# A fused attention and expert kernel: five raw weight buffers, loads one block further ahead, and one more set of keys and values ahead of the weights

## The chip, the cores and the metric

The kernel runs on one core of a Trainium2 chip. The time is device microseconds of one execution; several executions are timed and their median is taken. A separate execution is recorded by the hardware profiler, and all rows below are from that one.

## The reference

Three layers follow each other, all in fp32. The first is an attention with 16 heads (2 batches of 8) of 512 local and 32 global positions; a local position sees the global ones and its neighbours within 32. The second is a dense layer with three weight matrices, of which the largest product counts, and an output matrix. The third sends each token to one of eight experts. Cut to what matters:

```
out_l = softmax(q_l @ [k_g, k_l].T / 8, |pos difference| <= 32) @ [v_g, v_l]
out_g = softmax(q_g @ [k_g, k_l].T / 8) @ [v_g, v_l]
x = rows(out_g, out_l)                          # 1088 x 512
h = maximum(maximum(x @ w1, x @ w2), x @ w3)    # 512 x 768 each, float64 in memory
x = h @ w_out
e = argmax(x @ w_gate); y = gate * (relu(x @ w1[e]) @ w2[e])
```

## The kernel before

Everything up to the dense layer runs in one loop that is written out by hand. The heads are worked on in 16 sets of two heads and half a sequence; each set has one tile of queries and keys (`qk`, from `dma_qk`) and one of values (`rawv`, from `dma_v`), each with five buffers. A set has two units of 128 queries, so there are 32 units. The loop runs over steps s from -2 on. A step does one part of several units: scores, maximum and exponentials of unit s+2, the transpose of unit s (`u_trans` on TensorE, and `u_thi`, its copy `ph` on ScalarE), the product with the values of unit s-1 (`u_pv`), and the transposed output of unit s-2 (`x_out`). Steps 1, 5, 9 and so on also do scores of global positions (`g_scores`). The scores have one buffer (`ps_s`), so those of the next unit wait for the maximum of the last. `SEQ` lists the order of these parts in a step; each engine takes its instructions in the order in which the loop writes them. `idles` gives the number of matmuls on zeros (`warm`) that a step adds for TensorE.

The dense layer's weights are float64 in memory and are read as raw blocks of 128 x 512 (`raww`, 18 of them, three for each slice f of 128 hidden columns; then 6 of `w_out`). `split64` turns a block into a high and a low fp32 part: L337 on ScalarE reads the block, then L339, L342 and L345 on VectorE, L349 on ScalarE writes the high part, L352 and L354 on VectorE (L354 is the last to read the block), then L355 and L356 on GpSimd. The generator `w_stream` loads and splits the blocks in order. It is moved on by `take`: each advance does one pass, seven advances make one block, and the table `w_steps` says how many advances a step makes, divided over the places w0, w1 and w2 of `SEQ`. From step 10 on the dense layer's first matmuls (`moe_first`, L454) are mixed in.

All transfers of this part are issued by SP, which takes them in the order of the program, and one whose buffer is not free yet holds up those behind it. Ahead of the loop go qk of sets 0 to 2 and v of sets 0 and 1. The loop issues qk and v of one more set in every even step.

Of the kernel before, what the change touches and what calls it, by code (L numbers as in the profile page):

```python
# [7 lines left out]
F32 = mybir.dt.float32  # L8
# [4 lines left out]
I32 = mybir.dt.int32  # L13
# [6 lines left out]
P = 128  # L20
# [30 lines left out]
def tile_block(ctx: ExitStack, tc: tile.TileContext, qk, qg, v, vo, vg, w123, w_out, w_gate, w1, w2, consts, out):  # L51
# [16 lines left out]
    wp = wps.enter_context(tc.tile_pool(name="wp", bufs=2, side="right"))  # L68
# [14 lines left out]
    def warm(n):  # L83

        if n:
            o = ps_mm.tile([P, 512], F32, tag="mm", name="warm")
        for _ in range(n):
            nc.tensor.matmul(o[0:32], lhsT=idle, rhs=idle.unsqueeze(1).to_broadcast([P, 16, 32]), start=True, stop=True)
# [6 lines left out]
    def dma_qk(m):  # L95
        K[m] = ap.tile([P, 256 + KU], F32, tag="qk", bufs=5, name=f"qk{m}")
        nc.sync.dma_start(K[m], qk[m])

    def dma_v(m):
        V[m] = ap.tile([P, 8, P], F32, tag="rawv", bufs=5, name=f"rawv{m}")  # L100
        nc.sync.dma_start(V[m].rearrange("p t c -> p (t c)"), v[m])
# [69 lines left out]
    def u_scores(n):  # L171
        m, u = divmod(n, 2)
        ps = ps_s.tile([P, 2, 512], F32, tag="s", name=f"s{n}")
        PS_[n] = ps
        for j in range(2):
            t = K[m][64 * j : 64 * j + 64]
            for g in range(4):
                a = 256 + 32 * (5 * u + g)
                nc.tensor.matmul(ps[32 * g : 32 * g + 32, j, 0:P], lhsT=t[:, u * P + 32 * g : u * P + 32 * g + 32], rhs=t[:, a : a + P], start=True, stop=True)  # L179

    def u_max(n):
        m, u = divmod(n, 2)
        half = SETS[m][1]
        mk = mask[:, 0 if half == 0 and u == 0 else (2 if half == 1 and u == 1 else 1), :]
        nm = ap.tile([P, 2], F32, tag="nm", bufs=4, name=f"nm{n}")
        if u == 0:
            SS[m] = ap.tile([P, 2, 4], F32, tag="ssum", bufs=3, name=f"ss{m}")
        ssum = SS[m][:, 0, 2 * u : 2 * u + 2]
        sm = sms[n % NSM]
        SM[n] = (sm, nm, ssum)  # L190
        ps = PS_[n]
        for j in range(2):
            nc.vector.tensor_tensor_reduce(sm[:, j], ps[:, j, 0:P], mk, scale=-0.125, scalar=3.0e38, op0=ALU.add, op1=ALU.min, accum_out=nm[:, j : j + 1])  # L193
# [9 lines left out]
    def u_recip(n):  # L203
        if n % 2:
            t = SS[n // 2]
            nc.vector.reciprocal(t[:, 0], t[:, 1])

    def u_trans(n):
        sm = SM[n][0]
        pt = ps_t.tile([P, 2, P], F32, tag="pt", name=f"pt{n}")  # L210
        for j in range(2):
            nc.tensor.transpose(pt[:, j], sm[:, j], ident)
        PT_[n] = [pt]

    def u_thi(n):
        ph = ap.tile([P, 2, P], F32, tag="ph", name=f"ph{n}")
        nc.scalar.copy(ph, PT_[n][0])
        PT_[n].append(ph)

    def u_pv(n):  # L220
        m, u = divmod(n, 2)
        po = ps_v.tile([P, 2, 64], F32, tag="pv", name=f"pv{n}")
        _, ph = PT_.pop(n)
        for j in range(2):
            for g in range(4):
                nc.tensor.matmul(po[32 * g : 32 * g + 32, j], lhsT=ph[:, j, 32 * g : 32 * g + 32], rhs=V[m][:, 4 * u + g, 64 * j : 64 * j + 64], start=True, stop=True)
        xq = ap.tile([P, 2, 64], F32, tag="xq", bufs=3, name=f"xq{n}")
        nc.vector.tensor_tensor(xq, po, SM.pop(n)[2].unsqueeze(2).to_broadcast([P, 2, 64]), op=ALU.mult)
        PV_[n] = xq
# [127 lines left out]

    def dma_w(src, name):
        if wide:
            raw = wp.tile([P, 512, 2], I32, tag="raww", bufs=3, name=name)  # L360
            nc.sync.dma_start(raw.rearrange("p n t -> p (n t)"), src.bitcast(I32))
        else:
            raw = wp.tile([P, 512], F32, tag="raww", bufs=3, name=name)
            nc.sync.dma_start(raw, src)
        return raw

# [10 lines left out]
    def w_stream():  # L377

        todo = [("w", f, i) for f in range(NF) for i in range(3)] + [("o", f, 0) for f in range(NF)]
        raw = {}  # L380

        def load(k):
            if k < len(todo):
                kind, f, i = todo[k]
                raw[k] = dma_w(w123[f, i] if kind == "w" else w_out[f * P : (f + 1) * P], f"raw{kind}{f}{i}")

        load(0)
        load(1)
        yield
        load(2)  # L390
        old = iter(())
        for k in range(len(todo) + 1):

            new = (split64 if wide else split32)(raw.pop(k), *todo[k]) if k < len(todo) else iter(())
            next(old, None)
            yield
            next(new, None)
            yield
            next(old, None)
            if k:  # L400
                load(k + 2)
            yield
            for _ in range(4):
                next(new, None)
                yield
            old = new
# [54 lines left out]
    def take(gen, n):  # L461
        for _ in range(n):
            if next(gen, StopIteration) is StopIteration:
                return False
        return True
# [110 lines left out]
    ws = w_stream()  # L576
    NSET = len(SETS)
# [6 lines left out]
    def moe_stream():  # L584
        for g, f, at in ORDER:
            for _ in moe_first(f, *(WIN1[g])):
                yield at if at < 99 else 99 + f / 10
# [14 lines left out]
    GDVE = 6  # L602
    MM = (7, 4, 2, 1)

    w_steps = {-2: 1, 1: 2, 2: 1, 3: 2, 4: 2, 5: 1, 6: 2, 7: 1, 8: 1, 9: 1, 10: 6, 11: 5, 12: 5, 13: 3, 14: 2, 15: 3, 16: 7, 17: 3, 18: 1, 19: 5, 20: 4, 21: 3, 22: 1, 24: 4, 26: 6, 27: 3, 28: 1, 29: 1, 30: 5, 31: 4, 32: 2, 33: 2}
    idles = {-2: 4, 0: 1, 4: 3, 6: 1, 9: 1, 10: 1, 11: 1}

    GQ = {17: (0, 0), 21: (0, 1), 28: (1, 0), 31: (1, 1)}
# [1 line left out]
    mstream = None  # L610
    dma_qk(2)
    dma_v(1)
    for s in range(-2, NU + 6):
        live, ahead = 0 <= s < NU, 0 <= s + 2 < NU
        if s == 10:
            mstream = Stream(moe_stream())
        pull = (lambda n: mstream.pull(n, s)) if mstream else (lambda n: None)
        nw = w_steps.get(s, 0)
        for c_ in SEQ[0 if s < 14 else 1].split():
            if c_ == "scores" and ahead:  # L620
                u_scores(s + 2)
            elif c_ == "trans" and live:
                u_trans(s)
                u_thi(s)
            elif c_ == "max" and ahead:
                u_max(s + 2)
            elif c_ == "recip" and 0 <= s + 1 < NU:
                u_recip(s + 1)
            elif c_ == "pv" and 0 <= s - 1 < NU:
                u_pv(s - 1)  # L630
            elif c_ == "out" and 0 <= s - 2 < NU:
                x_out(s - 2)
            elif c_ == "exp" and ahead:
                u_exp(s + 2)
            elif c_ == "idle":
                warm(idles.get(s, 0))
            elif c_ == "quad":
                if s in GQ:
                    globs.append(g_quad(*GQ[s]))
                globs = [g for g in globs if next(g, StopIteration) is not StopIteration]  # L640
            elif c_ == "glob" and ahead and s % 4 == 1:
                g_scores((s - 1) // 2)
            elif c_ == "gcopy" and ahead and s % 4 == 1:
                g_copies((s - 1) // 2)
            elif c_[0] == "w":
                take(ws, (nw + int(c_[1])) // 3)
            elif c_[0] == "m" and c_ != "max":
                pull(MM[int(c_[1])])

        if s % 2 == 0:  # L650
            m = (s + 6) // 2
            if 3 <= m < NSET:
                dma_qk(m)
            if 2 <= m - 1 < NSET:
                dma_v(m - 1)
        if s == 11:
            load_qg(1)
        if s + 1 in GQ:
            dma_vg(*GQ[s + 1])
        if s == 28:  # L660
            routing_start()
        if s == 30:
            nc.sync.dma_start(out.rearrange("(p i) (j c) -> p (i j) c", p=64, c=P), zero[0:64].unsqueeze(1).to_broadcast([64, NT * DM // 64 // P, P]))
    k = 0
# [20 lines left out]
    k = 0  # L685
# [161 lines left out]
    def load(j, k):  # L847

        if j < NJ:
            kw = {} if j < 2 else {"cond": nsp[j] > 0}  # L850
            if k < 4:
                nc.sync.dma_start(raw_of(j, k), w1v[bass.ds(ereg[j], 1), k].rearrange("a p f -> (a p) f"), **kw)
            else:
                nc.sync.dma_start(raw_of(j, k), w2v[bass.ds(ereg[j], 1), k - 4].rearrange("a p i f -> (a p) i f"), **kw)
# [485 lines left out]
```

## Time and profile before

| what | value |
|---|---|
| median of 3 runs | 327.69 us (327.64 to 328.4) |
| the profiled execution's own time | 329.9 us |
| its span, first to last instruction | 328.1 us |
| busy in the span: TensorE / VectorE / ScalarE / GpSimd | 309.8 / 235.7 / 181.3 / 148.6 us |
| mean granted TensorE clock | 0.974 of full |

The busy times are sums over stages with different limits. A TensorE row counts as busy for as long as its matmuls last, also where they last longer at a lower clock. The granted clock is given as a share of 2.4 GHz: 1.00 is that level and 0.50 is 1.2 GHz.

### The profile page before, as it was taken

The page shows a single profiled execution, that of the slowest core. Times are in us where ns is not written, and L with a number is a line of the kernel's source. Part 1 is how long each engine was busy: PE and PEld are TensorE (multiplying, and loading weights), DVE is VectorE, ACT ScalarE, POOL GpSimd, SP SyncE. Part 2 cuts the span into 40 slices and gives each one's busy share as a digit, 9 for nine tenths or more (in the row PEclk, how much of TensorE's full clock was granted, in tenths as well). Part 3 has the DMA queues.
Part 4 walks back from the last instruction along what each step waited for, and adds up shares of the span by engine and source line. Part 5 has one row for each costly group of instructions (what it writes and reads, how often), then busy time and mean ns, then how long its engine had stood idle before and what let it go on. Part 6 is the DMA issues. An engine that isn't in the chain of part 4 may idle for free. (4 is left out here: it accounts for less than half of the span.)

```text
span 328.1 us, 8717 instructions
## 1 busy us (share of the span) xinstructions
PE 309.8 (94%) x3280; PEld 264.3 (81%) x3280; DVE 235.7 (72%) x600; ACT 181.3 (55%) x457; POOL 148.6 (45%) x164
## 2 busy tenths in 40 slices
PE   7699868999999999999999999999899999999993
PEld 2355746778887899999999999999799777788762
DVE  2569988796688827998996001765879799999881
ACT  4668477768757522433443121346532689889860
POOL 1128958593674814676888000142000357831131
PEclk9869796999999999999999999999999999999999
DMA  7947777486253962243310011469756189999921
GB/s 243 413 162 274 262 262 249 160 303 212 80 193 125 193 155 66 66 130 128 130 64 3 0 65 64 146 237 346 231 170 256 53 312 399 395 405 399 390 81 32
DMA packets 27656, 64.43 MB, mean 196 GB/s; under 512 B 3018, under 2 KB 8140, under 8 KB 27600
## 3 DMA queue, kind: packets, MB, share of 16 engines
q1 hardware_dynamic: 26304, 59.91, 52.9%
q0 software_dynamic: 1296, 3.82, 3.1%
q8 instruction: 30, 0.49, 0.6%
q14 instruction: 26, 0.21, 0.2%
HBM read 60.95 MB, written 7.27 MB: 208 GB/s over the span
## 5 line engine op out<-in xcount | busy, mean ns | idle before, releaser
L454 PE MATMUL h<-xh,wh 128*128 128x256 f32 (+1 forms) x288 | 85.3, 296 | 0.5 <-DVE hA L441 0.5
L454 PE MATMUL h<-xl,wh 128*128 128x256 f32 (+1 forms) x288 | 85.5, 297 | 0.0
L454 PE MATMUL h<-xh,wl 128*128 128x256 f32 (+1 forms) x288 | 85.5, 297 | 0.0
L454 PEld LDWEIGHTS h<-xh,wh 128*128 128x128 f32 x288 | 55.6, 193 | 1.2 <-DVE hA L441 0.7
L454 PEld LDWEIGHTS h<-xh,wl 128*128 128x128 f32 x288 | 55.9, 194 | 0.8 <-issue 0.7
L454 PEld LDWEIGHTS h<-xl,wh 128*128 128x128 f32 x288 | 55.9, 194 | 0.4 <-issue 0.2
L444 POOL TENSOR_TENSOR hTl<-hA,hTh 128x256 fp32r<-128x256 f32 (+1 forms) x24 | 19.3, 806 | 55.8 <-ACT hTh L443 55.7
L239 POOL CAST xh<-xs 128x128 fp32r<-128x128 f32 x32 | 13.1, 408 | 37.0 <-ACT xs L237 37.0
L859 DVE TENSOR_TENSOR w2l<-rawb,w2h 128x1024 fp32r<-128x1024 f32 x23 | 27.3, 1214 | 2.0 <-ACT w2h L858 2.0
L443 ACT CAST hTh<-hA 128x256 fp32r<-128x256 f32 (+1 forms) x24 | 10.0, 416 | 33.6 <-DVE hA L441 33.5
L739 PE MATMUL x<-hTl,wo_h 128*128 128x256 f32 (+1 forms) x96 | 28.3, 294 | 0.0
L198 ACT ACTIVATE sm<-sm,nm 128x128 f32<-128x128 f32 x64 | 25.3, 399 | 5.3 <-DVE nm L193 5.2
L441 DVE TENSOR_TENSOR hA<-hA,h 128x256 f32<-128x256 f32 (+1 forms) x48 | 20.7, 432 | 10.3 <-PE h L454 8.5
L739 PE MATMUL x<-hTh,wo_l 128*128 128x256 f32 (+1 forms) x96 | 27.9, 291 | 0.0
L739 PE MATMUL x<-hTh,wo_h 128*128 128x256 f32 (+1 forms) x96 | 27.8, 289 | 0.0
L355 POOL TENSOR_TENSOR ct<-ct,wh 128x512 f32<-128x512 f32 x18 | 25.8, 1432 | 1.3 <-DVE ca L352 0.9
L193 DVE CUSTOM_DVE_ANT_0 sm<-s,mask 128x128 f32<-128x128 f32 x64 | 15.9, 285 | 13.8 <-PE s L179 9.2
L942 PE MATMUL py<-w2h,hhl 128*128 128x512 f32 x96 | 25.5, 395 | 0.2 <-DVE idsall L573 0.2
L356 POOL TENSOR_TENSOR wl<-ct,ca 128x512 fp32r<-128x512 f32 x18 | 24.3, 1352 | 2.0 <-DVE ca L354 0.7
L859 DVE TENSOR_TENSOR w1l<-rawb,w1h 128x1024 fp32r<-128x1024 f32 x20 | 23.7, 1216 | 1.7 <-ACT w1h L858 1.6
L858 ACT CAST w2h<-rawb 128x1024 fp32r<-128x1024 f32 x23 | 23.4, 1050 | 1.8 <-DMA rawb<-in_w_dram 1.8
L817 POOL DMA_INDIRECT xg<-x2d,idsall x7 | 14.8, 2120 | 16.0 <-PE xp L829 14.8
(232 smaller groups left out, 723.3 us busy)
## 6 DMA issues: line engine op xcount, KB each, us to landing
rawb<-in_w_dram SPq DMA_DIRECT2D x51, 512.0 KB
raww<-in_w_dram SPq DMA_DIRECT2D x18, 512.0 KB
rawv<-in_v_dram SPq DMA_DIRECT2D x16, 512.0 KB
qk<-in_qk_dram SPq DMA_DIRECT2D x16, 320.0 KB
rawo<-in_w_out_dram SPq DMA_DIRECT2D x6, 512.0 KB
rw<-in_w_dram SPq DMA_DIRECT2D x5, 512.0 KB
out_dram<-zero SPq DMA_DIRECT2D x1, 2176.0 KB
rawg<-in_vo_dram SPq DMA_DIRECT2D x4, 512.0 KB
```

What stands on the lines that cost most here:

```text
L193: nc.vector.tensor_tensor_reduce(sm[:, j], ps[:, j, 0:P], mk, scale=-0.125, scalar=3.0e38, op0=ALU.add, op1=ALU.min, accum_out=nm[:, j : j ...
L198: nc.scalar.activation(sm[:, j], sm[:, j], AF.Exp, bias=nm[:, j : j + 1], scale=-1.0, accum_out=ssum[:, j : j + 1])
L355: nc.gpsimd.tensor_tensor(tf, tf, hi.bitcast(F32), op=ALU.subtract)
L356: nc.gpsimd.tensor_tensor(lo, tf, b.bitcast(F32), op=ALU.add)
L441: nc.vector.tensor_tensor(hA[:, :T], hA[:, :T], ph[:, :T], op=ALU.max)
L444: nc.gpsimd.tensor_tensor(hl[:, f_, c0 : c0 + T], hA[:, :T], dst.bitcast(F32), op=ALU.subtract)
L454: nc.tensor.matmul(ph[:, :T], lhsT=w_[:, a], rhs=x_[:, c, c0 : c0 + T], start=n == 0, stop=n == 11)
L739: nc.tensor.matmul(po[:, :T], lhsT=w_[:, f, d * P : (d + 1) * P], rhs=h_[:, f_, c0 : c0 + T], start=k == 0, stop=k == 17)
L817: nc.gpsimd.indirect_dma_start(out=xg[t if j == 0 else j % 2], out_offset=None, in_=src, in_offset=bass.IndirectOffsetOnAxis(ap=IDS[j][0:n ...
L858: nc.scalar.copy(h_, raw_of(j, k))
L859: nc.vector.tensor_tensor(l_, raw_of(j, k), h_.bitcast(F32), op=ALU.subtract)
L942: nc.tensor.matmul(py[0:nt], lhsT=a[:, c, a0 : a0 + nt], rhs=w_[:, c], start=i == 0, stop=i == 23)
```

## The change

Raw weight blocks have five buffers where they had three. `w_stream` issues its first three loads in three advances, in place of two, and then loads block k+3 where it loaded k+2. The first two advances are made ahead of the loop: block 0 behind qk 2 and v 1, then qk 3 and v 2, then block 1. The loop issues qk and v of each later set one even step earlier. The first entries of `w_steps` are spread more evenly (2 advances in each of steps 2 to 9, 4 in 10 and 11); the first pass of block 0 comes with the fifth advance where it came with the third, and two advances are made ahead of the loop, so that by the end of step 11 both kernels have done the same passes, and each later step does what it did.

```diff
-            raw = wp.tile([P, 512, 2], I32, tag="raww", bufs=3, name=name)
+            raw = wp.tile([P, 512, 2], I32, tag="raww", bufs=5, name=name)
...
         load(0)
+        yield
         load(1)
         yield
         load(2)
+        yield
...
-            if k:
-                load(k + 2)
+            load(k + 3)
...
-    w_steps = {-2: 1, 1: 2, 2: 1, 3: 2, 4: 2, 5: 1, 6: 2, 7: 1, 8: 1, 9: 1, 10: 6, 11: 5, 12: 5, 13: 3, 14: 2, 15: 3, 16: 7, 17: 3, 18: 1, 19: 5, 20: 4, 21: 3, 22: 1, 24: 4, 26: 6, 27: 3, 28: 1, 29: 1, 30: 5, 31: 4, 32: 2, 33: 2}
+    w_steps = {1: 1, 2: 2, 3: 2, 4: 2, 5: 2, 6: 2, 7: 2, 8: 2, 9: 2, 10: 4, 11: 4, 12: 5, 13: 3, 14: 2, 15: 3, 16: 7, 17: 3, 18: 1, 19: 5, 20: 4, 21: 3, 22: 1, 24: 4, 26: 6, 27: 3, 28: 1, 29: 1, 30: 5, 31: 4, 32: 2, 33: 2}
...
     dma_qk(2)
     dma_v(1)
+    take(ws, 1)
+    dma_qk(3)
+    dma_v(2)
+    take(ws, 1)
...
-            m = (s + 6) // 2
-            if 3 <= m < NSET:
+            m = (s + 8) // 2
+            if 4 <= m < NSET:
                 dma_qk(m)
-            if 2 <= m - 1 < NSET:
+            if 3 <= m - 1 < NSET:
                 dma_v(m - 1)
```

SP's queue, from the last transfer but one that both kernels issue alike (`qk3` is the tile of set 3, `rawv2` that of set 2; `raww00` to `raww02` are raw blocks 0 to 2, `raww10` is block 3). Before:

```order
L101 DMA rawv1_147<-in_v_dram 128x1024
L361 DMA raww00_164<-in_w123_dram 128x1024
L361 DMA raww01_166<-in_w123_dram 128x1024
L97 DMA qk3_211<-in_qk_dram 128x640
L101 DMA rawv2_213<-in_v_dram 128x1024
L361 DMA raww02_254<-in_w123_dram 128x1024
L97 DMA qk4_299<-in_qk_dram 128x640
L101 DMA rawv3_301<-in_v_dram 128x1024
L97 DMA qk5_389<-in_qk_dram 128x640
L101 DMA rawv4_391<-in_v_dram 128x1024
L361 DMA raww10_485<-in_w123_dram 128x1024
L97 DMA qk6_489<-in_qk_dram 128x640
```

The same place of SP's queue with the change:

```order
L361 DMA raww00_149<-in_w123_dram 128x1024
L97 DMA qk3_151<-in_qk_dram 128x640
L101 DMA rawv2_153<-in_v_dram 128x1024
L361 DMA raww01_155<-in_w123_dram 128x1024
L97 DMA qk4_215<-in_qk_dram 128x640
L101 DMA rawv3_217<-in_v_dram 128x1024
L361 DMA raww02_261<-in_w123_dram 128x1024
L97 DMA qk5_303<-in_qk_dram 128x640
L101 DMA rawv4_305<-in_v_dram 128x1024
L361 DMA raww10_341<-in_w123_dram 128x1024
L97 DMA qk6_392<-in_qk_dram 128x640
```

qk 3 and v 2 have moved in front of block 1, and one pair of qk and v now stands between any two blocks.

ScalarE's queue in steps 0 to 3, where L337 first reads block 0 (`nm4` is the maximum of unit 4, `pt2` the transposed block of unit 2). Before:

```order
L217 COPY ph1_241<-pt1_238 128x256
L198 ACTIVATE sm0_124,ss1_198<-sm0_124,nm3_233 128x128 x2
L201 ACTIVATE ss1_198<-ss1_198 128x4
L337 ACTIVATE ca_259<-raww00_164 128x512
L217 COPY ph2_277<-pt2_274 128x256
L237 COPY xs0_292<-pxq0_290 128x128
L198 ACTIVATE sm1_125,ss2_271<-sm1_125,nm4_270 128x128 x2
L217 COPY ph3_318<-pt3_315 128x256
```

The same place with the change:

```order
L217 COPY ph1_245<-pt1_242 128x256
L198 ACTIVATE sm0_124,ss1_202<-sm0_124,nm3_237 128x128 x2
L201 ACTIVATE ss1_202<-ss1_202 128x4
L217 COPY ph2_279<-pt2_276 128x256
L237 COPY xs0_294<-pxq0_292 128x128
L198 ACTIVATE sm1_125,ss2_273<-sm1_125,nm4_272 128x128 x2
L337 ACTIVATE ca_301<-raww00_149 128x512
L217 COPY ph3_322<-pt3_319 128x256
```

L337 has moved behind the copies of unit 2 and the exponentials of unit 4.

VectorE's queue in step 10, from L354 of block 1 to L345 of block 2 (`nm13<-s13` is the maximum of unit 13). Before:

```order
L354 SCALAR_TENSOR_TENSOR ca_477<-raww01_166,ca_477 128x512
L206 RECIPROCAL ss5_541<-ss5_541 128x4
L339 TENSOR_SCALAR ca_669<-ca_669 128x512
L342 TENSOR_SCALAR ca_669<-ca_669 128x512
L193 ISA sm1_125,nm13_696<-s13_687,mask_112 128x128
L193 ISA nm13_696 128x1
L193 ISA sm1_125,nm13_696<-s13_687,mask_112 128x128
L193 ISA nm13_696 128x1
L345 SCALAR_TENSOR_TENSOR ct_699<-raww02_254,ca_669 128x512
```

The same place with the change:

```order
L354 SCALAR_TENSOR_TENSOR ca_483<-raww01_155,ca_483 128x512
L228 TENSOR_TENSOR xq9_674<-pv9_665,ss4_458 128x128
L339 TENSOR_SCALAR ca_635<-ca_635 128x512
L206 RECIPROCAL ss5_548<-ss5_548 128x4
L342 TENSOR_SCALAR ca_635<-ca_635 128x512
L345 SCALAR_TENSOR_TENSOR ct_687<-raww02_261,ca_635 128x512
L193 ISA sm1_125,nm13_704<-s13_695,mask_112 128x128
L193 ISA nm13_704 128x1
L193 ISA sm1_125,nm13_704<-s13_695,mask_112 128x128
L193 ISA nm13_704 128x1
```

L345 of block 2 has moved in front of unit 13's maximum. TensorE's order is the same in both kernels.

## Rows read from the trace of the kernel before

**Rows 1.** The view by stretches: busy us (instructions) of each engine, granted clock, DMA.

```profile
core 0: us, PE busy (x) PEld busy (x) DVE busy (x) ACT busy (x) POOL busy (x), PEclk, DMA share, GB/s
6.00:12.00 6.00, 4.51 (x120) 2.64 (x120) 3.55 (x22) 3.83 (x17) 0.00 (x0) 1.00 1.03 402
12.00:15.20 3.20, 1.14 (x27) 0.62 (x20) 1.60 (x7) 3.08 (x14) 1.54 (x4) 0.91 1.01 405
15.20:21.80 6.60, 6.58 (x89) 3.35 (x89) 2.78 (x14) 2.29 (x8) 0.74 (x2) 0.53 0.71 276
...
29.30:42.00 12.70, 11.26 (x190) 8.34 (x190) 11.75 (x35) 7.76 (x30) 10.26 (x12) 0.87 0.75 256
...
60.00:100.00 40.00, 39.77 (x730) 33.86 (x729) 30.50 (x114) 29.82 (x110) 24.54 (x37) 1.00 0.50 170
```

**Rows 2.** The timeline of TensorE: start, us, instruction, idle before it and releaser.

```profile
6.68 0.45 PE L179 MATMUL s<-qk 64*32 64x128 f32 x16 [0.72 <-DVE nm L193]
...
10.25 0.45 PE L179 MATMUL s<-qk 64*32 64x128 f32 x16 [0.74 <-PE pv L226]
10.64 0.44 PE L212 MATMUL pt<-cst,sm 128*128 128x128 f32 x2
...
11.63 0.45 PE L179 MATMUL s<-qk 64*32 64x128 f32 x16
12.73 0.44 PE L212 MATMUL pt<-cst,sm 128*128 128x128 f32 x2 [0.66 <-ACT ph L217]
...
15.22 0.69 PE L179 MATMUL s<-qk 64*32 64x128 f32 x16 [1.43 <-DMA qk<-in_qk_dram]
...
21.85 0.45 PE L179 MATMUL s<-qk 64*32 64x128 f32 x16
...
24.91 0.45 PE L179 MATMUL s<-qk 64*32 64x128 f32 x16
...
29.31 0.45 PE L179 MATMUL s<-qk 64*32 64x128 f32 x16
...
34.75 0.45 PE L179 MATMUL s<-qk 64*32 64x128 f32 x16 [1.25 <-issue]
```

**Rows 3.** The view by stretches again, in half microseconds.

```profile
14.50:15.00 0.50, 0.00 (x0) 0.00 (x0) 0.23 (x1) 0.47 (x3) 0.47 (x1) 0.62 1.01 400
...
21.50:22.00 0.50, 0.49 (x16) 0.33 (x17) 0.47 (x3) 0.07 (x1) 0.00 (x0) 1.00 0.00 0
```

**Rows 4.** The timeline of ScalarE.

```profile
11.75 0.67 ACT L337 ACTIVATE ca<-raww 128x512 f32<-128x512 f32 x1 [1.18 <-DMA raww<-in_w_dram]
12.32 0.36 ACT L217 COPY ph<-pt 128x256 f32<-128x256 f32 x1
```

**Rows 5.** The list of waits, whole run: total us, times, longest us.

```profile
PE s L179 <- DMA qk<-in_qk_dram: 1.4, 1, 1.4
ACT ca L337 <- DMA raww<-in_w_dram: 1.2, 1, 1.2
```

**Rows 6.** The list of SP's waits, 0 to 60 us.

```profile
SPq L361 <- DVE ca L354: 41.0, 7, 12.0
```

**Rows 7.** The timeline of SP's queue.

```profile
24.11 0.33 SPq L361 DMA_DIRECT2D raww<-in_w_dram  x1
```

**Rows 8.** DMA issues: count and size of one.

```profile
raww<-in_w_dram SPq DMA_DIRECT2D x18, 512.0 KB
...
qk<-in_qk_dram SPq DMA_DIRECT2D x16, 320.0 KB
```

**Rows 9.** VectorE's groups by line, 22 to 54 us: busy us, mean ns.

```profile
L342 DVE TENSOR_SCALAR ca<-ca 128x512 int32<-128x512 int32 x5 | 5.3, 1061 | 0.0
L345 DVE SCALAR_TENSOR_TENSOR ct<-raww,ca 128x512 int32<-128x512 int32 x5 | 5.0, 1008 | 0.1
```

**Rows 10.** Lines 342 and 345, whole run: shortest, median and longest in ns.

```profile
L342 DVE TENSOR_SCALAR ca<-ca x15: 397/867/1397, 14.3 to 134.8; 128x512 int32<-128x512 int32 x15
...
L345 DVE SCALAR_TENSOR_TENSOR ct<-raww,ca x15: 678/693/1643, 17.4 to 136.5; 128x512 int32<-128x512 int32 x15
```

**Rows 11.** The timeline of VectorE.

```profile
32.86 1.37 DVE L342 TENSOR_SCALAR ca<-ca 128x512 int32<-128x512 int32 x1
```

More of the change, by code (lines that the diff above doesn't have):

```diff
@@ L359, in dma_w @@
         if wide:
-            raw = wp.tile([P, 512, 2], I32, tag="raww", bufs=3, name=name)
+            raw = wp.tile([P, 512, 2], I32, tag="raww", bufs=5, name=name)
             nc.sync.dma_start(raw.rearrange("p n t -> p (n t)"), src.bitcast(I32))
         else:
-            raw = wp.tile([P, 512], F32, tag="raww", bufs=3, name=name)
+            raw = wp.tile([P, 512], F32, tag="raww", bufs=5, name=name)
             nc.sync.dma_start(raw, src)
```

## The prediction

> **What bounds the kernel now.** I read the stages first. From 60 to 100 us TensorE is busy 39.77 of 40 us at the full clock [rows 1]; whatever is won before that stage moves it and all that hangs on it forward. The time to be had lies ahead of it. There three stretches stand out [rows 1]. From 12.0 to 15.2 us TensorE works 1.14 of 3.2 us. From 15.2 to 21.8 us it is "busy" 6.58 of 6.60, but at a granted clock of 0.53 with VectorE, ScalarE and GpSimd at 2.78, 2.29 and 0.74: that is work at the 1.2 GHz level, not much work. From 29.3 to 42 us VectorE is busy 11.75 of 12.70 and sets the pace.
>
> Then the matmul stream [rows 2]. Each row "s<-qk x16" is the scores of one attention unit; the one at 6.68 is the third of the run, unit 2. Unit 4 is at 10.25, 6 at 15.22, 8 at 21.85, 10 at 24.91, 12 at 29.31, 14 at 34.75. Unit 6 is the first to read set 3, and it waits 1.43 us for that set's transfer. The half-us windows [rows 3] show what the clock did: nothing runs from 14.5 to 15.0, the granted clock falls in that half us (0.62) and is back at 1.00 at 21.5. So one late transfer costs twice: the wait, and 6.6 us at the lower level.
>
> Next ScalarE [rows 4]: its first split pass (L337, on raw block 0) stands in front of the copy of unit 2's transposed block and waits 1.18 us for block 0's transfer; so the copy starts at 12.32, and the next transpose on TensorE (12.73) waits 0.66 us for it [rows 2].
>
> Over the whole run these are the only waits of an engine for qk and raw weights that the list names [rows 5]: one each, 1.4 and 1.2 us. SP's queue, on the other hand, waits 41.0 us up to 60 us, at L361, for the pass that frees a raw block [rows 6]; its fourth block goes out only at 24.11 [rows 7]. These waits delay transfers, yet no engine is seen waiting for what was delayed after 15.22.
>
> **The change part by part.** *Five buffers and one block further ahead.* Removed: SP's waits at L361. Since no engine waits for a raw block but the first [rows 5], I take 0 for this by itself. Bounds: 0, and the 1.2 us of that single wait, counted below. What covers it is the block in hand: blocks 1 and 2 are already in when block 0 is split. Without that cover a late block would cost what block 0 did, 1.2 us. Queued behind a waiting L361 were qk and v of later sets; those now go out on time too.
>
> *Set 3 in front of raw block 1.* In the SP rows set 3's qk now has raw block 0 right ahead of it, where it had blocks 0 and 1. Sizes are 512 KB (0.524 MB) for a raw block or a v, 320 KB (0.328 MB) for a qk [rows 8]. The transfers move 405 GB/s at that point [rows 1]. Before, block 0 was in at 11.75 (L337 starts [rows 4]) and qk 3 came 0.852 MB behind it: 2.10 us by bytes, but 15.22 - 11.75 = 3.47 us by the trace, 1.37 us more. Now it is 0.328 MB behind: 0.81 us by bytes. So it is in at 12.56 by bytes alone, or 12.56 + 1.37 = 13.93 if the extra stays. Which of the two, no row says.
>
> The Trainium skill, "DMA: Bandwidth & Descriptors", section "Queues, rings and completion order", has each DMA engine consume its descriptors in ring order, with completion not guaranteed in that order. By ring order alone qk 3 would be in at 12.56 and the sum below would be 0.4 us larger; the 3.47 us of the trace is longer than that.
>
> *The first split pass moves one step back.* In the ScalarE rows L337 now stands behind the exponentials of unit 4, so the copy for unit 2 no longer waits. Its transpose starts at 10.64 and lasts 0.44 [rows 2], so the copy can start at about 11.2 and end (0.36 us [rows 4]) at about 11.6; the transpose of unit 3 then follows unit 5's scores (11.63) at 12.0 in place of 12.73. What followed it took until 13.8 (15.22 less the wait of 1.43), which becomes 13.1. So unit 6 starts between 13.1 (chain) and 13.93 (transfer): 13.5, a gain of **1.7 us** (1.3 to 2.1).
>
> *The clock.* TensorE then stands for 0 to 0.8 us before unit 6, not 1.43 after another 0.66. Between 6 and 12 us it kept the full clock with 4.51 of 6.00 us busy [rows 1]. I take it that it keeps it here. Units 6 to 8 took 6.63 us (15.22 to 21.85). The same two steps at the full clock took 3.57 us (unit 2 to 4) and 4.40 us (unit 10 to 12), each with one group of global scores as here [rows 2]. Unit 6's step has three warming matmuls and a split pass, so I take the longer: 6.63 - 4.40 = **2.2 us**; bounds 0 (the clock falls anyway) and 3.1.
>
> *Would the next transfers then be late?* Unit 8 would come at 13.5 + 4.4 = 17.9, unit 10 at 21.0, unit 12 at 25.4. Behind block 0 the SP rows give 1.70, 3.08 and 4.46 MB up to and with qk 4, 5 and 6: at 405 GB/s 4.2, 7.6 and 11.0 us, so 16.0, 19.4 and 22.7, and with the extra 1.37 us 17.3, 20.7 and 24.1. All are in time, qk 5 by 0.3 us in the worse count. 0 us, up to 0.5 of loss.
>
> *Moved passes.* From step 4 to step 11 the passes of blocks 0 to 2 change places on VectorE: L342 and L345 of block 1 come a step earlier, and in step 10 L345 of block 2 now stands in front of unit 13's max. The sum of work is the same, and beyond step 11 VectorE's, ScalarE's and TensorE's order is as before. A pass that is pulled forward may meet GpSimd's L355 and L356: L342 means 1061 ns and L345 1008 ns from 22 to 54 us [rows 9], against 397 and 678 at their shortest [rows 10]. One of each more under that overlap loses 0.66 + 0.33 = 1.0 us; one of each less gains as much. VectorE's order does not tell which, so I take 0, with 1.0 to both sides.
>
> The Trainium skill, "GPSIMD Engine Reference", section "Specifications", says that GpSimd shares its SBUF interfaces with VectorE and lists contention with two-port or two-input VectorE work; the two means of rows 9 agree. It speaks against the change, since it puts L339, L342 and L345 right behind L354, which releases GpSimd; it gives no price.
>
> **The sum.** 1.7 + 2.2 + 0 + 0 = 3.9 us. The profiled execution lasted 329.9 us with a span of 328.1, 2.2 us above the median of 327.69, so I carry the difference over: 327.7 - 3.9 = **323.8 us**. It is kept to the end since from 60 us on work, not time, sets when things start.
>
> **Rivals.** *The wait shrinks, the clock still falls.* For it: a gap of up to 0.8 us remains, and the stretch before it is thin. Against: gaps of 0.72 and 0.74 us in front of units 2 and 4 did no harm [rows 2]. Then 1.7 us alone: 326.0 us.
>
> *Given back in the VectorE stage.* The order from unit 13 on is kept, but the stage from 29.3 us has gaps and a fall of the clock of its own (mean 0.87 [rows 1]); where an early start only meets work of GpSimd at a worse moment, the gain goes there: about 327.7 us. Also here: the change frees SP, and nobody waited for SP.
>
> *Slower: unit 13's max.* TensorE already stands 1.25 us before unit 14, at 34.75 [rows 2]: the one score buffer is not free, since unit 13's max comes behind an L342 of 1.37 us [rows 11]. Now L345 stands in front of that max as well: 0.68 to 1.64 us more [rows 10]. With the two passes above (1.0) VectorE is then 2.6 us late, and if TensorE's longer gap keeps its clock low for as long as after 15 us (up to 3.1 us lost there), 5.7 us are lost against 3.9 won: 1.8 more than before, 329.5 us. The clock decides: below a gap that brings it down, 2.6 us at most are lost, and the time stays under 326.5. Behind the max wait the scores of unit 14 and the exponentials of unit 13.
>
> **How the numbers follow.** A difference of 0.3%, 1.0 us, is about what a measurement of this kernel can tell from none. Forecast 0.50 (own range 321.5 to 325.7: gains of 1.3 + 2.2 - 1.0 - 0.5 and 2.1 + 3.1 + 1.0), clock falls anyway 0.17, given back 0.15, slower 0.14, and 0.04 for anything else. Faster by over 0.3%: the first two and a little of the third, 0.68; within: 0.15; slower: 0.17 with the rest. The range 321.8 to 328.2 leaves out the slower case and the best of the forecast's own.
>
> **What the profile of the changed kernel would show.** Right: no wait of scores for qk near 13 us; unit 6 at 13.1 to 13.9; L337 behind unit 4's exponentials without a wait; granted clock 1.00 from 12 to 22 us; unit 8 near 18, unit 12 near 25.4; SP's wait at L361 for L354 gone before 60 us; the 60 to 100 us stage as full as now, 4 us earlier. Wrong: a granted clock near 0.5 in 13 to 20 us (326.0); units 8, 10 or 12 waiting for qk; or units 12 to 14 further apart than now (12 to 14 took 5.44 us), above all a gap before unit 14 over 1.25 us.

## The result, and the profile after

The changed kernel takes 324.71 us (median of 20 executions, 323.93 to 329.05), the kernel before 327.9 us beside it (20 executions). The ratio is 0.9903, with a 95% interval of 0.9884 to 0.9921: 3.2 us faster, where 3.9 had been forecast. The profiled execution took 325.35 us, with a span of 323.6 us. The total is close. The terms behind it are not, as the experiments show, so part of that closeness is luck.

The view by stretches of the changed kernel, in the columns of [rows 1]:

```profile
6.00:12.00 6.00, 3.53 (x91) 2.07 (x95) 2.92 (x19) 3.58 (x16) 0.00 (x0) 1.00 0.99 380
12.00:15.20 3.20, 3.04 (x87) 1.81 (x86) 2.33 (x16) 2.90 (x12) 1.11 (x4) 1.00 1.04 412
15.20:18.00 2.80, 2.80 (x69) 1.59 (x58) 2.07 (x11) 2.04 (x10) 1.59 (x3) 1.00 1.02 405
18.00:24.00 6.00, 4.76 (x107) 2.50 (x107) 5.50 (x18) 5.48 (x23) 4.12 (x6) 1.00 1.03 404
24.00:30.00 6.00, 4.95 (x95) 3.37 (x96) 4.31 (x21) 3.45 (x13) 3.44 (x8) 0.72 1.03 400
...
60.00:100.00 40.00, 39.94 (x744) 34.23 (x731) 31.49 (x118) 31.13 (x113) 25.11 (x37) 1.00 0.58 178
...
92.00:142.00 50.00, 50.00 (x540) 48.25 (x539) 36.05 (x80) 20.93 (x60) 32.04 (x35) 1.00 0.46 126
```

As foreseen, TensorE now works 3.04 us from 12.0 to 15.2 us, where it had 1.14, and its clock stays at 1.00 up to 24 us. Not foreseen: from 24 to 30 us the mean granted clock is 0.72, so part of that stretch ran at the 1.2 GHz level. Its timeline shows what stands ahead of that (the first row is a transpose, the others are the scores of units 4, 6, 8, 10, 11, 12 and 14):

```profile
8.18 0.41 PE L212 MATMUL pt<-cst,sm 128*128 128x128 f32 x2 [1.02 <-DMA cst<-in_consts_dram]
...
11.20 0.45 PE L179 MATMUL s<-qk 64*32 64x128 f32 x16 [0.74 <-DVE sg L272]
...
14.16 0.45 PE L179 MATMUL s<-qk 64*32 64x128 f32 x16 [0.16 <-DVE xq L228]
...
18.68 0.45 PE L179 MATMUL s<-qk 64*32 64x128 f32 x16 [0.48 <-PE pxq L234]
...
21.73 0.45 PE L179 MATMUL s<-qk 64*32 64x128 f32 x16
25.05 0.68 PE L179 MATMUL s<-qk 64*32 64x128 f32 x16 [1.81 <-DVE nm L193]
28.89 0.45 PE L179 MATMUL s<-qk 64*32 64x128 f32 x16
...
34.52 0.45 PE L179 MATMUL s<-qk 64*32 64x128 f32 x16 [1.61 <-issue]
```

Against [rows 2], unit 6 is 1.06 us earlier, unit 8 is 3.17, unit 10 is 3.18, and unit 12 only 0.42. No row names qk as what it waited for. Ahead of unit 11, TensorE stands 1.81 us for unit 10's maximum (the two other traces with this order of passes, after_again and three_bufs below, have 1.76 and 1.82 us there). VectorE's timeline shows what that maximum (24.41) was behind:

```profile
21.82 1.26 DVE L339 TENSOR_SCALAR ca<-ca 128x512 f32<-128x512 f32 x1
23.11 1.37 DVE L342 TENSOR_SCALAR ca<-ca 128x512 int32<-128x512 int32 x1
24.41 0.28 DVE L193 CUSTOM_DVE_ANT_0 sm<-s,mask 128x128 f32<-128x128 f32 x1
...
94.16 0.17 DVE L152 CAST val_all<-cst 128x10 bf16<-128x10 f32 x1
94.23 0.32 DVE L153 CAST iota_b<-iota 128x128 bf16<-128x128 f32 x1
```

The last two rows are wanted further below. Both passes, L339 and L342, run while GpSimd does L355 and L356, as its timeline shows:

```profile
21.52 1.27 POOL L355 TENSOR_TENSOR ct<-ct,wh 128x512 f32<-128x512 f32 x1
22.87 1.33 POOL L356 TENSOR_TENSOR wl<-ct,ca 128x512 fp32r<-128x512 f32 x1
```

SP's wait at L361 up to 60 us, the answer to [rows 6]:

```profile
SPq L361 <- DVE ca L354: 14.1, 6, 4.0
```

The prediction had this wait gone; 14.1 of the 41.0 us are left.

**Where the traces part.** From each trace I took the starts of units 6, 12, 20 and 31 (scores, L179) and of the 17th cast to a high weight part (L349 or L350 on ScalarE, which belongs to the dense layer's last weight blocks), and the span's end. Names other than before and changed are those of the experiments. In us:

| trace | unit 6 | unit 12 | unit 20 | unit 31 | cast 17 | unit 31 to cast 17 | end |
|---|---|---|---|---|---|---|---|
| before | 15.22 | 29.31 | 58.57 | 95.67 | 146.49 | 50.82 | 328.1 |
| before_again | 15.20 | 27.16 | 55.70 | 93.20 | 144.04 | 50.84 | 325.6 |
| start_only | 14.87 | 26.97 | 55.43 | 92.53 | 143.37 | 50.84 | 324.2 |
| start_again | 14.17 | 26.13 | 53.60 | 91.93 | 142.76 | 50.83 | 323.8 |
| start_third | 14.27 | 26.29 | 54.83 | 91.44 | 142.16 | 50.72 | 323.2 |
| three_bufs | 14.70 | 28.65 | 55.97 | 92.86 | 143.71 | 50.85 | 324.6 |
| buf5_only | 15.28 | 29.36 | 57.26 | 94.59 | 143.76 | 49.17 | 325.2 |
| iota_early | 15.42 | 28.77 | 57.34 | 94.16 | 143.33 | 49.17 | 324.7 |
| passes_back | 14.07 | 26.02 | 57.70 | 94.31 | 143.48 | 49.17 | 324.8 |
| changed | 14.16 | 28.89 | 56.81 | 93.41 | 142.57 | 49.16 | 323.6 |
| after_again | 13.62 | 27.86 | 55.16 | 92.09 | 141.25 | 49.16 | 322.6 |
| late_passes_back | 14.32 | 26.28 | 54.77 | 91.57 | 140.74 | 49.17 | 321.9 |
| late_again | 14.85 | 26.81 | 55.85 | 92.34 | 141.50 | 49.16 | 322.9 |
| warm_fill | 14.01 | 25.95 | 54.03 | 91.26 | 140.40 | 49.14 | 322.2 |

The stretch from unit 31 to cast 17 has two lengths only, about 50.8 us (50.72 to 50.85) and about 49.2 (49.14 to 49.17). The kernels with five buffers have the shorter one; of those with three, iota_early alone has it. Rows of before that the prediction left out say why. SP's timeline (`iota` is a constant of 128 x 128 that the third layer's routing needs; its transfer is issued in step 28):

```profile
92.08 0.33 SPq L361 DMA_DIRECT2D raww<-in_w_dram  x1
...
93.40 0.43 SPq L149 DMA_DIRECT2D iota<-in_consts_dram  x1
```

The list of SP's waits of before, 84 to 94 us, and then VectorE's and TensorE's timelines:

```profile
SPq L361 <- DVE ca L354: 25.6, 3, 13.1
```

```profile
97.70 0.33 DVE L153 CAST iota_b<-iota 128x128 bf16<-128x128 f32 x1 [1.21 <-DMA iota<-in_consts_dram]
97.95 0.21 DVE L154 CAST lowtri_b<-cst 128x128 bf16<-128x128 f32 x1
98.09 0.28 DVE L193 CUSTOM_DVE_ANT_0 sm<-s,mask 128x128 f32<-128x128 f32 x1
```

```profile
102.24 0.44 PE L212 MATMUL pt<-cst,sm 128*128 128x128 f32 x2 [0.70 <-ACT ph L217]
...
113.75 0.40 PE L454 MATMUL h<-xh,wh 128*128 128x288 f32 x1 [0.49 <-DVE hA L441]
```

A raw block whose buffer is not free holds SP's queue, and behind it stands the small transfer that VectorE's queue will need. VectorE waits 1.21 us with unit 31's maximum behind it; the exponentials and the transposed block come late, and TensorE, which had no other gap from 95 to 142 us, stands 0.70 and 0.49 us. In the changed kernel L153 follows the cast before it without a wait (the last rows of VectorE's timeline above), TensorE is busy for 50.00 of the 50 us from 92 to 142 (the last row of the view by stretches), and SP's timeline has the transfer 8 us ahead of its use:

```profile
86.11 0.42 SPq L149 DMA_DIRECT2D iota<-in_consts_dram  x1
```

### The profile page after: what moved, and what is told of

Same layout as the page of the kernel before. It is cut to its first block, busy times and chain, and to the rows that moved or that the text cites. A ratio compares the mean times of both kernels' runs of the same rounds, so it can differ in the third digit from the quotient of the medians.

```text
span 323.6 us, 8712 instructions
## 1 busy us (share of the span) xinstructions
PE 307.3 (95%) x3280; PEld 263.5 (81%) x3280; DVE 233.8 (72%) x600; ACT 181.1 (56%) x457; POOL 147.6 (46%) x164
## 5 line engine op out<-in xcount | busy, mean ns | idle before, releaser
L239 POOL CAST xh<-xs 128x128 fp32r<-128x128 f32 x32 | 14.1, 439 | 32.5 <-ACT xs L237 32.4
L356 POOL TENSOR_TENSOR wl<-ct,ca 128x512 fp32r<-128x512 f32 x18 | 24.6, 1365 | 2.6 <-DVE ca L354 1.4
L355 POOL TENSOR_TENSOR ct<-ct,wh 128x512 f32<-128x512 f32 x18 | 25.0, 1391 | 1.3 <-DVE ca L352 0.9
```

The lines of the kernel that those rows point to most:

```text
L355: nc.gpsimd.tensor_tensor(tf, tf, hi.bitcast(F32), op=ALU.subtract)
L356: nc.gpsimd.tensor_tensor(lo, tf, b.bitcast(F32), op=ALU.add)
```

## The experiments

Two theories. The first is the prediction's: the gain comes from the start, through the earlier set 3, the first pass a step later, and the clock that this keeps. The second: it comes from SP's queue, which five buffers free ahead of the transfer of iota. Ratios are to the kernel before, timed beside it on the same chip, with 95% intervals.

**buf5_only.** The kernel before with the buffers alone:

```diff
-            raw = wp.tile([P, 512, 2], I32, tag="raww", bufs=3, name=name)
+            raw = wp.tile([P, 512, 2], I32, tag="raww", bufs=5, name=name)
```

> The kernel before with five raw buffers and nothing else; the order on every engine and queue is unchanged. Theory 1 (the prediction's: no engine waits for what SP holds up): no change, ratio to before 0.998 to 1.002. Theory 2 (from the trace of the changed kernel: a constant that SP issues behind a held-up weight load, waited for 1.2 us at 97 us, comes in time when SP is free): 1.0 to 1.6 us less, ratio 0.995 to 0.997, and no wait of VectorE for that constant.

Measured: 325.65 us (12 executions) against 327.7, ratio 0.9953 [0.9927, 0.998]. L153 has no wait, and unit 6 stays at 15.28. The buffers alone are worth about 1.5 us; the prediction had 0.

**start_only.** The kernel before with one part of the transfers alone: qk 3 and v 2 ahead of raw block 1, passes and buffers as before. On SP's queue only raw block 1 changes its place, and no other engine's order changes; qk and v of the later sets stay in their even steps.

```diff
         load(0)
+        yield
         load(1)
...
-    w_steps = {-2: 1, 1: 2, 2: 1, 3: 2, ...
+    w_steps = {1: 2, 2: 1, 3: 2, ...
...
+    take(ws, 1)
+    dma_qk(3)
+    dma_v(2)
+    take(ws, 1)
...
             m = (s + 6) // 2
-            if 3 <= m < NSET:
+            if 4 <= m < NSET:
                 dma_qk(m)
-            if 2 <= m - 1 < NSET:
+            if 3 <= m - 1 < NSET:
                 dma_v(m - 1)
```

> The kernel before with raw block 1 issued behind qk 3 and v 2 and nothing else. Theory 1: no wait of unit 6 for qk, full clock from 14 to 22 us, unit 8 at 18 to 19 us in place of 21.85, and as the split passes stay where they were, nothing is given back: 2.5 to 3.5 us less, ratio 0.989 to 0.992. Rival (the stage from 24 us gives an early start back whatever the order of its passes): unit 8 as early, but unit 16 within 0.7 us of before, ratio 0.997 to 1.0.

Measured: 328.56 us (12 executions, 326.02 to 331.16), ratio 1.0047 [1.0016, 1.0079]: not faster. Two of the twelve took 331 us; the other ten have a median of 328.03, against 327.7, so that it is slower is not shown. Its trace does show an early start (unit 12 at 26.97), but that execution was the shortest of the twelve. This move alone gains nothing.

**passes_back.** The changed kernel with the `w_steps` of before, so that against before only SP's order and the buffers are changed. The expectation says that the loads keep the changed order; they do not quite. They hang on the advances too, and blocks 2 and 3 are each issued one pair of qk and v earlier than in the changed kernel (block 2 right behind block 1).

```diff
-    w_steps = {1: 1, 2: 2, 3: 2, 4: 2, 5: 2, 6: 2, 7: 2, 8: 2, 9: 2, 10: 4, 11: 4, 12: 5, ...
+    w_steps = {-2: 1, 1: 2, 2: 1, 3: 2, 4: 2, 5: 1, 6: 2, 7: 1, 8: 1, 9: 1, 10: 6, 11: 5, 12: 5, ...
```

> The changed kernel with the advances of before (the same passes in the same steps as before); the loads keep the changed order and five buffers. Theory 1: the moved passes are worth 0, so as the changed kernel, ratio 0.989 to 0.992. Theory 2 (the changed kernel loses 2 to 3 us where unit 10's maximum stands behind L339 and L342, and its clock falls at 25 us): no fall at 25 us, unit 12 at 26 to 27 us, 1 to 2 us less than the changed kernel, ratio 0.984 to 0.988.

Measured: 325.86 us (12 executions), ratio 0.9946 [0.9918, 0.9974], the same as the buffers alone. Its trace has unit 6 at 14.07 and unit 12 at 26.02, and is behind the changed kernel's again by unit 20. Where it falls back, TensorE's timeline and the view by stretches show:

```profile
29.79 0.24 PE L226 MATMUL pv<-rawv,ph 128*32 128x64 f32 x1 [2.60 <-issue]
```

```profile
27.60:29.80 2.20, 0.01 (x1) 0.01 (x1) 0.00 (x0) 0.16 (x1) 0.00 (x0) 1.00 1.01 400
30.00:36.00 6.00, 6.00 (x63) 3.46 (x63) 5.56 (x13) 3.10 (x12) 5.05 (x7) 0.55 0.97 338
```

The last of the sixteen matmuls of a product with the values comes 2.60 us after the fifteenth, and TensorE waits for nothing that the profile shows ("issue"). Hardly any other engine works in that time, while the transfers go on at 400 GB/s; then the granted clock is 0.55. The same place has a gap of 0.58 us in late_passes_back and at most 0.58 in the other traces. What TensorE waits for there is not shown.

**late_passes_back.** The changed kernel, with the passes of blocks 1 and 2 back in their steps of before and those of block 0 left as changed.

```diff
-    w_steps = {... 7: 2, 8: 2, 9: 2, 10: 4, 11: 4, ...
+    w_steps = {... 7: 1, 8: 1, 9: 1, 10: 6, 11: 5, ...
```

> The changed kernel with the passes of steps 7 to 11 where they were before and those up to step 6 as changed. Theory 1: as the changed kernel, ratio 0.989 to 0.992. Theory 2: no gap before unit 11 and no fall of the clock at 25 us, unit 12 at 26 to 27 us, 1 to 2 us less than the changed kernel, ratio 0.984 to 0.988.

Measured: 324.21 us (6 executions), ratio 0.9914 [0.988, 0.9947]. The long gap ahead of unit 11 is gone and unit 12 starts at 26.28, 2.6 us earlier than in the changed kernel; the median is only 0.5 us below the changed kernel's, which was not timed beside it, and within the interval.

**three_bufs.** The changed kernel with three buffers, and block k+2 loaded where it loads k+3.

```diff
-            raw = wp.tile([P, 512, 2], I32, tag="raww", bufs=5, name=name)
+            raw = wp.tile([P, 512, 2], I32, tag="raww", bufs=3, name=name)
...
-            load(k + 3)
+            if k:
+                load(k + 2)
```

> The changed kernel with three raw buffers and block k+2 loaded where it loads k+3: only the look-ahead is undone, the orders on the engines stay as changed. Theory 1 (the prediction's: the early transfers and the first pass give the gain, the buffers nothing): as the changed kernel, 0.989 to 0.992 of before. Theory 2 (the buffers give 1.5 us as in the run with five buffers alone, the moved passes 1.4 us, the early transfers nothing): 0.994 to 0.998, and VectorE's wait for the constant near 97 us is back.

Measured: 326.92 us (12 executions) against 327.86, ratio 0.9986 [0.9956, 1.0015]. L153 waits 1.2 us again. So transfers and passes without the buffers lie between 1.4 us won and 0.5 us lost; the prediction gave them 3.9 won.

**before_again** and **start_again.** The kernel before and start_only, one more profile each, with no edit.

> The kernel before once more, for a second trace. If the stretch at the low clock from 15 to 22 us is fixed, it is there again, with unit 8 at 21.5 to 22 us. If it comes and goes from one execution to the next, the mean granted clock is nearer the 0.984 that most executions show, and one of the low stretches (15, 35 or 53 us) is missing.

> The kernel with block 1 behind qk 3 and v 2 alone, for a second trace: the first was the shortest of its 12 executions. If the early transfers cost time in the usual execution, this trace is 2 to 4 us longer and shows where; with the low clock as the cause, its mean is 0.971 to 0.979 against 0.989, and the units fall back at a gap of TensorE between 25 and 60 us.

Measured: spans of 325.6 and 323.8 us. The profile of before on which the prediction rests is not what every execution does. In before_again (TensorE's timeline, then the view by stretches; units 6 and 8):

```profile
15.20 0.45 PE L179 MATMUL s<-qk 64*32 64x128 f32 x16 [1.01 <-DVE ca L342]
...
19.68 0.45 PE L179 MATMUL s<-qk 64*32 64x128 f32 x16 [0.48 <-PE pxq L234]
```

```profile
12.00:15.20 3.20, 2.19 (x54) 1.23 (x53) 2.40 (x13) 3.06 (x13) 1.31 (x4) 1.00 1.04 412
15.20:21.80 6.60, 6.12 (x142) 3.38 (x142) 4.74 (x22) 4.74 (x19) 2.21 (x6) 1.00 0.74 288
```

The clock does not fall: units 6 to 8 take 4.48 us, where [rows 2] show 6.63. Unit 6 starts at the same time, and it waits for qk here too, if less long (1.01 us). The row names L342, whose output the scores do not read, but by the semaphore events in the trace the last part of qk 3 is in at 15.06 us (15.09 in before), just ahead of it. The wait is shorter because the units before come later (unit 4 at 11.36, where [rows 2] have 10.25). Whether the stretch at the 1.2 GHz level occurs differs from execution to execution of the same kernel.

**warm_fill.** late_passes_back with 14 more matmuls on zeros (4 + 4 + 3 + 3, where the expectation counts 13), to keep TensorE's clock up between 20 and 60 us.

```diff
-    idles = {-2: 4, 0: 1, 4: 3, 6: 1, 9: 1, 10: 1, 11: 1}
+    idles = {-2: 4, 0: 1, 4: 3, 6: 1, 9: 1, 10: 1, 11: 5, 15: 4, 16: 3, 17: 3}
```

> The changed kernel with the passes of steps 7 to 11 where they were before, and with 13 more warming matmuls on TensorE: four behind step 11, four in step 15 and three each in steps 16 and 17, in front of the gaps that precede its low clock at 33 and 50 us. If the low clock there costs what it lasts at half speed (3 and 3 us), 1 to 3 us less than without them, 0.983 to 0.989 of before. If VectorE sets that stage's end anyway, no difference to it: 0.990 to 0.993.

Measured: 324.49 us (9 executions), ratio 0.9917 [0.9887, 0.9948], the same as without. The view by stretches, 20 to 60 us, of late_passes_back and of warm_fill:

```profile
20.00:60.00 40.00, 33.60 (x602) 24.56 (x603) 34.84 (x114) 29.08 (x111) 30.57 (x40) 0.91 0.86 315
```

```profile
20.00:60.00 40.00, 35.77 (x634) 24.55 (x633) 34.99 (x114) 29.25 (x111) 30.72 (x41) 0.96 0.88 327
```

The clock rose from 0.91 to 0.96 and the time did not change. VectorE is busy 34.8 and 35.0 of the 40 us. TensorE's own busy time rose by 2.17 us, in part through the added matmuls, so what the clock by itself would give is not shown.

**iota_early.** The kernel before, three buffers and all, with one transfer moved: iota in step 20 in place of step 28.

```diff
     def routing_start():
-        iota = ac.tile([P, P], F32, name="iota")
-        nc.sync.dma_start(iota, consts[:, NCONST - P : NCONST])
...
+        if s == 20:
+            iota_load()
```

> The kernel before, three buffers and all, with one edit: the 64 KB transfer of the routing constant iota, which SP's queue held behind a raw block that waited for its buffer, is issued in step 20 in place of step 28; no engine's order changes but SP's. Theory (the five buffers are worth time because they clear SP's queue ahead of this one small transfer): VectorE's wait at L153 is gone, the stage from unit 31's scores to the 17th cast at L349 or L350 takes 49.2 us in place of 50.8, and the time falls by about 1.7 us: ratio 0.993 to 0.997, as for the five buffers alone (0.9953). Rival (the five buffers give their time through the raw blocks themselves): the wait is gone but the stage keeps 50.8 us or the time stays, ratio 0.998 to 1.002.

Measured: 326.07 us (12 executions) against 327.96, ratio 0.9932 [0.9902, 0.9962]. In its VectorE timeline iota's cast (L156 in this kernel) follows its predecessor at once:

```profile
94.30 0.70 DVE L154 CAST val_all<-cst 128x10 bf16<-128x10 f32 x1
94.91 0.17 DVE L155 CAST val_all<-cst 128x10 bf16<-128x10 f32 x1
94.98 0.32 DVE L156 CAST iota_b<-iota 128x128 bf16<-128x128 f32 x1
```

SP still waits 39.0 us for its raw blocks up to 60 us here (41.0 in [rows 6]), and the stretch from unit 31 to cast 17 is 49.17 us. So a single transfer moved out from behind the held queue gives what five buffers give. That settles the second theory.

**after_again** and **late_again.** The changed kernel and late_passes_back, beside each other.

> The changed kernel once more, beside the version with the passes of blocks 1 and 2 later. Theory (the gap in front of unit 11 costs what its trace shows, 2.7 us of the lead): 1.5 to 2.5 us slower than late_again in the same call. Rival (the stretch up to unit 12 is made up later or is not the same in every execution): within 0.7 us of it. Its time against the kernel before: ratio 0.988 to 0.993.

> The changed kernel with the passes of blocks 1 and 2 later, once more: ratio 0.988 to 0.995 to the kernel before; by the first theory 1.5 to 2.5 us below after_again, by the rival within 0.7 us of it.

Measured: 325.01 us (11 executions, 324.39 to 326.31) and 324.09 us (6 executions, 323.12 to 324.8); ratios 0.9928 [0.9897, 0.9958] and 0.9888 [0.9853, 0.9923]. The difference is 0.9 us, between the two expectations. The intervals above are to the kernel before; worked out from the executions of the two kernels themselves, the means differ by 1.1 us, with a 95% interval of 0.4 to 1.8. The two traces do not show it (unit 12 at 27.86 and 26.81, but ends at 322.6 and 322.9 us). In late_again unit 6 waits for qk 3 again, behind the same early transfers, and the clock stays up:

```profile
14.85 0.45 PE L179 MATMUL s<-qk 64*32 64x128 f32 x16 [1.68 <-DMA qk<-in_qk_dram]
```

```profile
12.00:15.20 3.20, 1.52 (x51) 0.82 (x35) 1.23 (x6) 2.84 (x13) 1.48 (x4) 1.00 1.03 408
15.20:21.80 6.60, 6.12 (x139) 3.38 (x132) 5.53 (x26) 4.61 (x18) 2.41 (x6) 1.00 1.03 405
```

The VectorE rows of late_again show the order that keeps unit 11 on time, with the maximum of unit 10 between the two passes:

```profile
22.48 1.26 DVE L339 TENSOR_SCALAR ca<-ca 128x512 f32<-128x512 f32 x1
23.66 0.28 DVE L193 CUSTOM_DVE_ANT_0 sm<-s,mask 128x128 f32<-128x128 f32 x1
...
24.37 0.78 DVE L342 TENSOR_SCALAR ca<-ca 128x512 int32<-128x512 int32 x1
```

**start_third.** start_only, a third profile.

> The early transfers alone, a third profile, since both profiles so far are shorter than its usual execution. Theory (its usual execution loses the early lead again through stretches at the lower clock between units 12 and 20): a span of 326 us or more with unit 31's scores at or after 94 us, and the stage behind them as long as in the other profiles. Rival (the loss lies behind unit 31): unit 31 at 92 to 93 us and a longer stage behind it. A third short profile (span up to 324.5 us) leaves it open.

Measured: 323.2 us of span, unit 31 at 91.44. It leaves the question open, as said there.

## Why the prediction came out, step by step

**The step that failed** is "*Five buffers and one block further ahead* ... I take 0 for this by itself". It measured 1.5 us alone (buf5_only), and 2.2 us between three_bufs and the changed kernel (326.92 to 324.71, not timed side by side). The reason given, that no engine waits for a raw block but the first, is true. What is false is that "no engine is seen waiting for what was delayed after 15.22": the queue that the blocks hold up carries other transfers too, and the list of waits of before had the row for one of them, iota:

```profile
DVE iota_b L153 <- DMA iota<-in_consts_dram: 1.2, 1, 1.2
```

The prediction took from the list only the waits for qk and raw weights [rows 5], and its second rival says "nobody waited for SP". Between before and the changed kernel the wait costs 1.66 us in the stage from unit 31 to cast 17 (50.82 against 49.16). TensorE's two gaps make 1.19 of them; the other 0.47 are busy time (49.63 against 49.16 us for the same 533 matmuls), which no run explains.

**The start, 1.7 us.** L337 moved behind unit 4's exponentials, and unit 6 starts at 14.16 (13.62 in after_again) where 13.1 to 13.9 had been said. Against before that is 1.06 us, less than the 1.3 of the lower bound, with the start itself delayed by a 1.02 us wait for the constants, which put unit 4 0.95 us later than in [rows 2]; from unit 4 to unit 6 the gain is 4.97 - 2.96 = 2.0 us. But the transfer bounds unit 6 as well. By the semaphore events qk 3 is in at 14.03 in the changed kernel, 0.13 us ahead of unit 6, near the 13.93 of the prediction's second case, and at 12.28 in after_again, before its first, 12.56. In the ten traces with the early transfers it is in between 12.28 and 14.74, in the four without between 15.06 and 15.28. So the wait became shorter and did not always go (1.68 us in late_again). The step had the direction right and its size for some executions only.

**The clock, 2.2 us.** The price was right: between the two traces of before, one with the fall and one without, units 6 to 8 differ by 6.63 - 4.48 = 2.15 us. The change does remove this fall: from 15.2 to 21.8 us the granted clock is 1.00 in all ten traces with the early transfers. What failed is that the sum set the whole price against the median: without them the clock there is 0.53 in before, 0.56 in buf5_only, 0.74 in iota_early, but 1.00 in before_again. A change can't win back in the median what the usual execution may not lose. How often the fall occurs in unprofiled executions no run tells. In the 67 executions of before under 329.9 us that were timed beside the experiments, the 13 with a mean clock under 0.978 have a median of 329.05 us and the other 54 one of 327.51: stretches at the lower clock, wherever they lie, go with 1.5 us between executions.

**Both together, 3.9 us**, are tested by three_bufs, which has all of the change but the buffers: won 0.9 us between the medians, with an interval from 1.4 won to 0.5 lost. The early transfers gave nothing alone (start_only, with set 3 only), nor on top of the buffers (passes_back against buf5_only, 325.86 and 325.65), though passes_back has the 2.60 us gap of its own. This is the term that was too large, and the error on the buffers hid it: that the sum came within 0.7 us of the measured gain is luck.

**Later transfers, 0.** Right: no unit waits for qk 4 to 6 in the changed kernel.

**Moved passes, 0 with 1.0 to both sides.** They are two moves, and by these runs of opposite sign. Putting blocks 1 and 2 a step earlier did what the rival on unit 13's maximum described, three units earlier: L339 and L342 beside GpSimd in front of unit 10's maximum, a 1.81 us gap, a clock of 0.72, and 2.76 of the 3.18 us lead gone at unit 12. The sign that the prediction named for that rival is there too, though small: units 12 to 14 take 5.63 us (5.44 before), with a gap of 1.61 us in front of unit 14 (1.25 before). Taking that move back wins 0.5 us where the two were timed apart and 0.9 where they were timed side by side (0.4 to 1.8 by the means). The mean clock agrees: 0.966 to 0.984 in the eleven executions of after_again, 0.980 to 0.987 in the six of late_again. Leaving block 0's passes a step later, on the other hand, is what late_passes_back has over passes_back, timed side by side: 325.86 to 324.21, 1.65 us (by the means 1.6, with a 95% interval of 0.8 to 2.4). The same edit moves blocks 2 and 3 on SP's queue, so the two causes are not separated. In the traces passes_back is 0.26 us ahead at unit 12 and 2.93 behind at unit 20, and what lies between is the gap of 2.60 us (0.58 in late_passes_back) with the low clock behind it. Why it is worth that much with five buffers, while transfers and passes with three are worth next to nothing, the runs do not settle.

**Given back in the VectorE stage.** In part: late_passes_back is 2.6 us ahead of the changed kernel at unit 12 and 1.7 at the end of its trace, late_again 1.05 ahead of after_again and then 0.3 behind; in the median it is 0.5 to 0.9. After 60 us work, not time, sets the order, as said: of the changed kernel's 2.26 us lead at unit 31 nothing is lost, and 1.66 are added by iota.

So the account of the 3.2 us: 1.5 to 2.2 from SP's queue, shown twice (the ratios of buf5_only and iota_early, with 1.67 between the lengths in the traces); the rest, 1.0 to 1.7, came only with the moved advances (passes, and blocks 2 and 3 on SP's queue) on top of the early transfers, and is not separated further. What stays open too is why the usual execution of start_only (328.03 without the two at 331) is 2.0 us or more above its three profiled ones (326.02, 325.56, 324.97). Of those ten, the five with a mean clock of 0.979 or less took 328.4 to 330.8 us and the other five 326.0 to 327.7, so it goes with stretches at the lower clock, but no profile caught such an execution.

The best version found is late_passes_back: 324.21 and 324.09 us in its two sets of 6, against 324.71 and 325.01 for the changed kernel.

## What to carry to other kernels

When a change frees a queue, list everything that the queue carries, small constants too, and look in the list of waits for each; a transfer that costs nothing by its bytes can stand behind a load that waits for its buffer, and moving that one transfer may do what more buffers do. Before a stall of one profiled execution is priced against a median, take a second profile of the same kernel, and see whether the stall is there. Where a row names a releaser on which its instruction does not depend, see what else ended just then. When passes are moved in a written order, ask for each maximum on which TensorE waits what now stands in front of it, at every unit and not only where the order is most changed.

## What the runs showed of the hardware that was not expected

Two executions of one kernel differ in where TensorE falls to the 1.2 GHz level: from 15.2 to 21.8 us the granted clock was 0.53 in one trace of before and 1.00 in the other, where TensorE had worked 1.14 and 2.19 of the 3.2 us ahead of it. That work alone does not tell which it will be: it was 1.59 us in iota_early, where the clock then was 0.74, and 1.52 in late_again, where it stayed at 1.00.

A higher clock need not save time: between 20 and 60 us the mean rose from 0.91 to 0.96 with 14 matmuls on zeros, and the medians are 324.21 and 324.49 us. The added matmuls take TensorE's time themselves, so this is no price of the clock alone.

VectorE's passes did not slow down beside GpSimd by a share of their length: they ended with it. Between 20 and 54 us of the changed kernel eight passes at L339 and L342 begin while an L355 or L356 runs, and all eight end 0.28 to 0.29 us after it ends, however much of it was left. The rows of both engines above show two: 21.82 + 1.26 = 23.08 against 21.52 + 1.27 = 22.79, and 23.11 + 1.37 = 24.48 against 22.87 + 1.33 = 24.20. In late_again the later L342 meets only the last half microsecond of L356, as GpSimd's timeline there shows:

```profile
23.54 1.33 POOL L356 TENSOR_TENSOR wl<-ct,ca 128x512 fp32r<-128x512 f32 x1
```

It ends at 24.37 + 0.78 = 25.15, 0.28 us after 24.87. So the 0.397 and 1.397 us of [rows 10] are two cases of one rule. The Trainium skill, "SBUF — State Buffer", section "SBUF: two separate sides", calls the port pair that the two engines share an exclusive lock, held for a whole instruction, with the loser fully blocked. These rows agree with it in that no such pass ends before GpSimd's instruction does. The 0.28 us left behind that end are less than the 0.397 that L342 takes at its shortest, so they do not show the pass blocked from the start that the profile gives it. The 1.0 us to both sides in the prediction could have been worked out from L355's and L356's ends in place of means.
